# Attention in front of a feed-forward part, moved to the whole tensor array: zero-padded queries, P as the stationary operand, a ones column in V

## The chip, the cores and the metric

The kernel runs on one core of one Trainium2 chip. The metric is device time in microseconds (us), as the median of several executions. PE is the tensor engine (PEld its weight loads), ACT the scalar engine, DVE the vector engine and POOL the engine that issues most loads.

## The reference

There are 8 batches, 8 heads, 576 positions and 64 values a head. Heads 0 to 3 see a local window of 32 positions. Heads 4 to 7 see the earlier positions with the same remainder modulo 32. The attention output, 4608 tokens of 512 values, goes through a bilinear feed-forward part (FFN).

```python
scores = scale * np.matmul(q, k.transpose(0, 1, 3, 2))
mask_local   = (rel >= 0) & (rel < stride)                      # heads 0..3, stride = 32
mask_strided = (rel >= 0) & (pos[None, :] % stride == pos[:, None] % stride)
attn = softmax(where(mask, scores, -1e9));  o = attn @ v        # per batch and head
x = o.transpose(0, 2, 1, 3).reshape(4608, 512)
out = ((x @ w_a) * (x @ w_b)) @ w_out                           # 512 -> 1536 -> 512
```

## The kernel before

The FFN works in 9 tiles of 512 tokens: 12 groups of 8 matmuls (a and b), then 4 groups of 12 (y). pf is the product of a and b. The attention of batch b+1 is cut into steps that are issued between the FFN groups of tile b; the place behind one group is called a slot. A unit is half the positions of one pair of heads, 8 units a batch. Batch 0 has nothing to hide behind and forms the start. The order on PE is fixed by hand.

A head has 64 values, so each attention step used half of the array. Scores contract over 64 rows; transposes and P V write 64 columns. Two heads run beside each other, in the two halves.

```python
def step_S(b, u):                       # scores: two heads in two ROW halves (64*128)
    for i, (k0, q0, g) in enumerate(segs):
        for hh in range(2):
            d0 = 64 * hh
            nc.tensor.matmul(st[:M, hh, i*n:(i+1)*n], lhsT=kT[d0:d0+64, c, k0:k0+M],
                             rhs=qT[d0:d0+64, c, q0:q0+n], start=True, stop=True)
    # ... exp on ACT, mask by a bitwise and on DVE -> p

def step_V(b, u):                       # P V: two heads in two COLUMN halves (128*64)
    for hh in range(2):                 # row sums by a matmul with ones
        nc.tensor.matmul(dn[64*hh:64*hh+64, :W], lhsT=ones[:M], rhs=p[:M, hh], start=True, stop=True)
    # ... o[64*hh:64*hh+64, ...] = matmul(lhsT=vt, rhs=p): x comes out transposed
    nc.scalar.activation(ln, dn[:, :W], ACT.Ln)
    nc.scalar.activation(rc, ln, ACT.Exp, scale=-1.0)      # 1/sum
    nc.vector.tensor_mul(x[:, W*half:W*(half+1)], o[:, :W], rc)
# pools in PSUM: mm 4 banks, st 2, sm 2
```

The softmax here doesn't subtract the row's maximum and nothing guards it: scores larger than these inputs give would overflow.

## Time and profile before

| | before |
|---|---|
| time, median of 4 executions | 375.57 us (375.12 to 375.96) |
| span of the profiled execution | 374.7 us |
| PE busy | 358.7 us, 96% |
| an FFN tile with / without attention beside it | 39.95 / 31.08 us |
| a batch of attention on PE | 8.87 us |
| FFN's first matmul | 25.21 us |

The prediction below shows the lines for most of these rows. A few are from the timeline of PE (start, duration in us, engine, line, operation with its operands, rows*columns of the array in use, number of instructions, in brackets the wait before). The last is from the view of waits (engine, tile and line, what it waited for: us in total, times, longest).

```profile
24.83 0.45 PE L220 MATMUL sm<-p,vs 72*64 72x72 bf16 x8 [0.51 <-ACT ln L224]
...
67.77 0.82 PE L254 MATMUL mm<-xT,wa_sb 128*128 128x512 bf16 x3
69.36 0.38 PE L254 MATMUL mm<-xT,wa_sb 128*128 128x512 bf16 x1 [0.77 <-DVE xT L232]
```

```profile
PE mm L254 <- DVE xT L232: 0.8, 1, 0.8
```

The last P V of batch 0 begins at 24.83 and the FFN follows at 25.21, just 0.38 us later: its first three passes read x of heads 0 to 5, which was multiplied earlier. DVE finishes the last unit's x at 26.03, and the fourth pass, the first that needs it, comes at about 26.5. The wait of 0.8 us is the only long one outside the start. It lies at the boundary of tiles 0 and 1.

### The profile page before, as it was taken

What the parts mean: (1) busy time and instruction counts of PE and PEld (TensorE: products, weight loads), DVE (VectorE), ACT (ScalarE), POOL (GpSimd) and SP (SyncE); (2) the same over time, 40 slices, a digit from 0 to 9 for tenths busy, and PEclk for the clock granted to TensorE, in tenths of its full rate; (3) what the DMA queues carried; (4) which work ended last, traced back from release to release, by engine and by line L of the source; (5) the groups of instructions that cost most, each with busy time, mean ns of one, the idle gap of its engine ahead of it and who ended that gap; (6) DMA issues with size and microseconds to landing.
All of it is one profiled execution on the core that took longest, in us unless ns stands there. A gap on an engine that the chain in (4) does not pass through costs nothing.

```text
span 374.7 us, 7708 instructions
## 1 busy us (share of the span) xinstructions
PE 358.7 (96%) x3217; PEld 173.8 (46%) x3217; DVE 169.7 (45%) x299; ACT 178.6 (48%) x347; POOL 52.3 (14%) x72
## 2 busy tenths in 40 slices
PE   2789999999999999999999999999999999999995
PEld 2544454455444544444444544554445444444442
DVE  2653652465426652556245643655255513312421
ACT  1563764466526652666246643766166623312320
POOL 7833540013001110103000300000000000000000
PEclk9999999999999999999999999999999999999999
DMA  7999999845644194229414843000200020011002
GB/s 114 155 194 197 205 191 191 177 66 37 98 117 65 8 100 117 53 40 103 93 56 66 72 81 99 2 2 19 94 2 3 1 86 28 0 58 56 0 30 84
DMA packets 51730, 29.59 MB, mean 79 GB/s; under 512 B 28400, under 2 KB 47088, under 8 KB 51696
## 3 DMA queue, kind: packets, MB, share of 16 engines
q0 software_dynamic: 46512, 19.67, 43.2%
q1 hardware_dynamic: 5184, 9.44, 6.9%
q8 instruction: 25, 0.41, 0.4%
q14 instruction: 9, 0.07, 0.1%
HBM read 39.31 MB, written 9.44 MB: 130 GB/s over the span
## 4 chain that ended last, share of the span: by engine, by line
PE 93%; DMA 2%; POOL 1%; ACT 1%; DVE 1%; issue 1%; DVEq 0%; POOLq 0%
PE mm L254 52%; PE mm L265 25%; PE sm L166 5%; PE st L194 4%; PE sm L213 4%; PE sm L220 2%; DMA vl<-in_v_dram 2%; POOL k L116 0%; DVE y_sb L271 0%; POOL msl L73 0%; ACT rc L226 0%; DVE xT L232 0%; ACT ln L224 0%; POOL q L116 0%; PE mm L166 0%
## 5 line engine op out<-in xcount | busy, mean ns | idle before, releaser
L259 DVE TENSOR_TENSOR pf<-a_sb,mm 128x512 bf16<-128x512 f32 x108 | 74.3, 688 | 89.9 <-PE mm L254 89.9
L254 PE MATMUL mm<-xT,wa_sb 128*128 128x512 bf16 x432 | 113.6, 386 | 0.8 <-DVE xT L232 0.8
L254 PE MATMUL mm<-xT,wb_sb 128*128 128x512 bf16 x432 | 111.9, 382 | 0.0
L258 ACT COPY a_sb<-mm 128x512 f32<-128x512 f32 x108 | 63.2, 585 | 70.2 <-PE mm L254 70.2
L265 PE MATMUL mm<-wo_sb,pf 128*128 128x512 bf16 x432 | 96.3, 379 | 0.0
L254 PEld LDWEIGHTS <-wb_sb 128*128 128x128 bf16 x432 | 42.6, 99 | 52.9 <-issue 2.9
L265 PEld LDWEIGHTS <-pf 128*128 128x128 bf16 x432 | 40.9, 98 | 47.9
L254 PEld LDWEIGHTS <-wa_sb 128*128 128x128 bf16 x432 | 36.4, 98 | 38.4 <-issue 1.7
L199 ACT ACTIVATE p<-st 128x576 bf16<-128x576 f32 (+1 forms) x64 | 40.7, 635 | 17.5 <-PE st L194 17.4
L224 ACT ACTIVATE ln<-sm 128x288 f32<-128x288 f32 x64 | 26.3, 410 | 29.5 <-PE sm L213 29.5
L269 ACT COPY y_sb<-mm 128x512 f32<-128x512 f32 x18 | 10.5, 585 | 56.3 <-PE mm L265 56.3
L271 DVE COPY y_sb<-mm 128x512 f32<-128x512 f32 x18 | 12.5, 692 | 52.9 <-PE mm L265 52.9
L232 DVE TENSOR_TENSOR xT<-sm,rc 128x288 bf16<-128x288 f32 x32 | 20.4, 639 | 28.4 <-ACT rc L226 27.8
L226 ACT ACTIVATE rc<-ln 128x288 f32<-128x288 f32 x64 | 28.3, 443 | 2.0
L172 ACT COPY qT<-sm 128x576 bf16<-128x576 bf16 x28 | 17.8, 637 | 13.9 <-PE sm L166 13.9
L194 PE MATMUL st<-qT,kT 64*72 64x72 bf16 (+1 forms) x448 | 21.1, 212 | 0.6 <-ACT p L199 0.5
L213 PE MATMUL sm<-p,ones 72*64 72x288 bf16 (+1 forms) x128 | 21.1, 327 | 0.3 <-DVE p L205 0.3
L229 DVE TENSOR_TENSOR xT<-sm,rc 128x288 bf16<-128x288 f32 x32 | 14.6, 458 | 14.2 <-ACT rc L226 12.5
L116 POOL DMA_DIRECT2D q<-in_q_dram x16 | 11.7, 730 | 58.4 <-PE sm L166 53.7
L213 PEld LDWEIGHTS <-ones 72*64 72x64 bf16 (+1 forms) x128 | 7.3, 110 | 24.6 <-issue 21.2
L166 PEld LDWEIGHTS <-q 72*64 72x64 bf16 (+1 forms) x448 | 11.2, 117 | 15.9 <-issue 8.9
L129 POOL DMA_DIRECT2D vl<-in_v_dram x8 | 11.6, 1454 | 45.9 <-PE st L194 45.4
(41 smaller groups left out, 177.8 us busy)
## 6 DMA issues: line engine op xcount, KB each, us to landing
out_dram<-y_sb SPq DMA_DIRECT2D x36, 256.0 KB, 2.0
q<-in_q_dram POOLq DMA_DIRECT2D x16, 288.0 KB, 6.8
k<-in_k_dram POOLq DMA_DIRECT2D x16, 288.0 KB, 7.9
vl<-in_v_dram POOLq DMA_DIRECT2D x7, 384.0 KB, 6.8
vs<-in_v_dram POOLq DMA_DIRECT2D x8, 288.0 KB, 5.8
wa_sb<-in_moe_w_a_dram POOLq DMA_DIRECT2D x4, 384.0 KB, 11.6
wb_sb<-in_moe_w_b_dram POOLq DMA_DIRECT2D x4, 384.0 KB, 11.7
wo_sb<-in_moe_w_out_dram POOLq DMA_DIRECT2D x4, 384.0 KB, 13.5
```

The lines of the kernel that those rows point to most:

```text
L166: nc.tensor.transpose(tp[64 * hh:64 * hh + 64, r, :], src[:, 2 * cc + hh, r, :], ident[:n, :n])
L172: nc.scalar.copy(o, i_)
L194: nc.tensor.matmul(st[:M, hh, i * n:(i + 1) * n], lhsT=kT[d0:d0 + 64, c, k0:k0 + M], rhs=qT[d0:d0 + 64, c, q0:q0 + n], start=True, stop=True)
L199: nc.scalar.activation(p[:M], st[:M, :, :W], ACT.Exp, scale=scale)
L213: nc.tensor.matmul(dn[64 * hh:64 * hh + 64, :W], lhsT=ones[:M], rhs=p[:M, hh], start=True, stop=True)
L224: nc.scalar.activation(ln, dn[:, :W], ACT.Ln)
L226: nc.scalar.activation(rc, ln, ACT.Exp, scale=-1.0)
L232: nc.vector.tensor_mul(dst, o[:, :W].rearrange("d (r p) -> d p r", r=4), rc.rearrange("d (r p) -> d p r", r=4))
L254: nc.tensor.matmul(ps_, lhsT=w[:, f // FC, kk, 128 * (f % FC):128 * (f % FC + 1)], rhs=xT[:, kk, TTOK * t:TTOK * (t + 1)], start=(kk == 0) ...
L258: nc.scalar.copy(a_sb, ab[0])
L259: nc.vector.tensor_mul(pf[:, f, :], a_sb, ab[1])
L265: nc.tensor.matmul(y, lhsT=pf[:, f, 128 * j:128 * (j + 1)], rhs=wo_sb[:, f, :], start=(f == 0), stop=(f == FD - 1))
```

## The change

The intent is that every attention step but the local transposes uses the whole array. Then the array need not change between its modes (whole, row halves, column halves; each change is a gap of 93 to 97 ns in the trace before), and ln and 1/x leave ACT.

- Scores contract over all 128 rows, two heads of k at once, against queries in which the other head's rows are zero (`qz`).
- P becomes the stationary operand and V the moving one, with a 65th column of ones. The output has queries on partitions, and the row sum arrives as column 64.
- Each row is divided by its sum on DVE. The result must then be transposed into x, 28 transposes a batch.
- Strided q and k are transposed 128 values wide. V of the strided heads is loaded in 4 transfers, and buffers are redistributed.

```diff
-    pmm = ... bufs=4     psm = ... bufs=2
+    pmm = ... bufs=3     po = ... bufs=1 (2 banks)     ptp = ... bufs=1
 def step_S
-   matmul(st[:M, hh, ...], lhsT=kT[d0:d0 + 64, c, k0:k0 + M], rhs=qT[d0:d0 + 64, c, q0:q0 + n])
+   matmul(st[:M, j, ...],  lhsT=kT[:, c, k0:k0 + M],          rhs=qz[j][:, c, q0:q0 + n])
 def step_V
-   matmul(dn[...], lhsT=ones[:M], rhs=p[:M, hh])
-   matmul(o[64 * hh:64 * hh + 64, ...], lhsT=vt, rhs=p[:M, hh, i * n:(i + 1) * n])
-   ACT.Ln, ACT.Exp(scale=-1), tensor_mul into xT
+   matmul(ov[:, j, i, :], lhsT=p[:M, j, i * n:(i + 1) * n], rhs=vt)      # vt has D + 1 columns
+   reciprocal(rc, ov[:, :, :, D]);  tensor_mul(xn, ov[:, :, :, 0:D], rc)
+def step_X                                                               # new
+   transpose(tv[:, g, :], xn[:, g], ident)   for 6 or 8 pieces;  scalar.copy into xT
-   pf ... bufs=2;   batch t+1 begins with tile t (batch 1: behind FFN group 3)
+   pf ... bufs=1;   batch b begins two groups before tile b-1 (batch 1: group 2, doubled steps at 3 and 12)
```

More of the change, by code (lines that the diff above doesn't have):

```diff
@@ L20 @@
 PAD = 32
+VW = 80
 FC = 3
@@ L52 @@
     nat = ctx.enter_context(tc.tile_pool(name="nat", bufs=2))
-    kvp = ctx.enter_context(tc.tile_pool(name="kv", bufs=2))
     sb = ctx.enter_context(tc.tile_pool(name="sb", bufs=3))
     fsb = ctx.enter_context(tc.tile_pool(name="ffn", bufs=3))
-    pmm = ctx.enter_context(tc.tile_pool(name="pmm", bufs=4, space=bass.MemoryType.PSUM))
+    pmm = ctx.enter_context(tc.tile_pool(name="pmm", bufs=3, space=bass.MemoryType.PSUM))
     pst = ctx.enter_context(tc.tile_pool(name="pst", bufs=1, space=bass.MemoryType.PSUM))
-    psm = ctx.enter_context(tc.tile_pool(name="psm", bufs=2, space=bass.MemoryType.PSUM))
+    po = ctx.enter_context(tc.tile_pool(name="po", bufs=1, space=bass.MemoryType.PSUM))
+    ptp = ctx.enter_context(tc.tile_pool(name="ptp", bufs=1, space=bass.MemoryType.PSUM))
     nc.scalar.preload_act_table_set("natural_log_exp_and_others")
     ident = const.tile([128, 128], BF16)
-    ones = const.tile([128, 64], BF16)
+    qz_buf = [[const.tile([128, KD, S], BF16, name=f"qz{i}{j}") for j in range(2)] for i in range(2)]
+    vl_buf = [const.tile([128, HL * 6, VW], BF16, name=f"vl{i}") for i in range(2)]
+    vs_buf = [const.tile([NP, HL, RS, VW], BF16, name=f"vs{i}") for i in range(2)]
     mask_l = const.tile([128, 4, LW], I16)
@@ L74, in select, with consts @@
                                 channel_multiplier=cm)
-    def consts():
-        nc.vector.memset(ones, 1.0)
-        nc.vector.memset(msl, -1.0)
-        for kT in kT_buf:
-            nc.vector.memset(kT[:, 0:2, 0:PAD], 0.0)
+    def consts(i):
+        if i == 0:
+            nc.vector.memset(msl, -1.0)
+        nc.vector.memset(kT_buf[i][:, 0:2, 0:PAD], 0.0)
+        for j in range(2):
+            nc.vector.memset(qz_buf[i][j][64 * (1 - j):64 * (2 - j)], 0.0)
+        nc.vector.memset(vl_buf[i][:, :, D:D + 1], 1.0)
+        nc.vector.memset(vs_buf[i][:, :, :, D:D + 1], 1.0)
+        if i == 0:
+            nc.vector.memset(vl_buf[0][:PAD, 0, 0:D], 0.0)
     def mask_local():
@@ L119, in load_vl @@
     def load_vl(b):
-        t = nat.tile([128, HL * 6, D], BF16, tag="vl", name="vl")
+        t = vl_buf[b % 2]
         f = 0
@@ L124, in load_vl @@
             f = 1
-            nc.vector.memset(t[:PAD, 0, :], 0.0)
-            nc.gpsimd.dma_start(out=t[PAD:, 0, :], in_=v[0, 0, 0:LW, :])
+            nc.gpsimd.dma_start(out=t[PAD:, 0, 0:D], in_=v[0, 0, 0:LW, :])
         src = bass.AP(tensor=v.tensor, offset=(b * H * S + LW * f - PAD) * D,
                       ap=[[D, 128], [LW * D, HL * 6 - f], [1, D]])
-        nc.gpsimd.dma_start(out=t[:, f:, :], in_=src)
-        nats[b, "vl"] = t.rearrange("p (h w) d -> p h w d", h=HL)
+        nc.gpsimd.dma_start(out=t[:, f:, 0:D], in_=src)
     def load_vs(b):
-        t = nat.tile([NP, HL, RS, D], BF16, tag="vs", name="vs")
-        nc.gpsimd.dma_start(out=t, in_=v[b, HL:].rearrange("h (p r) d -> p h r d", r=RS))
-        nats[b, "vs"] = t
+        for h in range(HL):
+            nc.gpsimd.dma_start(out=vs_buf[b % 2][:, h, :, 0:D],
+                                in_=v[b, HL + h].rearrange("(p r) d -> p r d", r=RS))
     def load_w(src, dst, c):
@@ L147, in load_wo, with step_T @@
         )
-    qkT = {}
-    def step_T(b, c):
-        if b not in qkT:
-            qkT[b] = (kvp.tile([128, KD, S], BF16, tag="qT", name="qT"), kT_buf[b % 2])
-        R, n = (RS, NP) if c >= 2 else (RL, 96)
-        cc = c % 2
-        for i, nm in enumerate(("q", "k")):
-            src = nats[b, nm, c >= 2]
-            dst = qkT[b][i][:, c, :] if i == 0 else qkT[b][i][:, c, PAD:]
-            if b == 0:
-                tp = pmm.tile([128, R, n], BF16, tag="mm", name="mm")
-            else:
-                tp = psm.tile([128, R, n], BF16, tag="sm", name="sm")
-            for r in range(R):
-                for hh in range(2):
-                    nc.tensor.transpose(tp[64 * hh:64 * hh + 64, r, :], src[:, 2 * cc + hh, r, :], ident[:n, :n])
-            if c < 2:
-                o, i_ = dst.rearrange("d (p r) -> d p r", r=R), tp.rearrange("d r p -> d p r")
-            else:
-                o, i_ = dst, tp.rearrange("d r p -> d (r p)")
-            if i == 0 and b > 0:
-                nc.scalar.copy(o, i_)
-            else:
-                nc.vector.tensor_copy(o, i_)
+    def step_T(b, c, nm):
+        src = nats[b, nm, c >= 2]
+        if b == 0:
+            tp = pmm.tile([128, S], BF16, tag="mm", name="mm")
+        else:
+            tp = ptp.tile([128, S], BF16, tag="tp", name="tp")
+        if c < 2:
+            tv = tp.rearrange("d (r p) -> d r p", r=RL)
+            for r in range(RL):
+                for hh in range(2):
+                    nc.tensor.transpose(tv[64 * hh:64 * hh + 64, r, :], src[:, 2 * c + hh, r, :], ident[:96, :96])
+            perm = lambda t: t.rearrange("d (p r) -> d p r", r=RL)
+            tv = tv.rearrange("d r p -> d p r")
+        else:
+            tv = tp.rearrange("d (g p) -> d g p", p=NP)
+            sv = src.rearrange("p h (q r) d -> p h q (r d)", r=2)
+            for g in range(8):
+                nc.tensor.transpose(tv[:, g, :], sv[:, 2 * (c - 2) + g // 4, g % 4, :], ident[:NP, :NP])
+            perm = lambda t: t
+            tv = tp
+        if nm == "k":
+            nc.vector.tensor_copy(perm(kT_buf[b % 2][:, c, PAD:]), tv)
+        else:
+            for j in range(2):
+                pr = slice(64 * j, 64 * j + 64)
+                nc.scalar.copy(perm(qz_buf[b % 2][j][pr, c, :]), tv[pr])
@@ L176, in unit, with step_Tk, step_Tq @@
+    def step_Tk(b, c):
+        step_T(b, c, "k")
+    def step_Tq(b, c):
+        step_T(b, c, "q")
     def unit(u):
         c, half = u // 2, u % 2
-        if c < 2:
-            ws = range(3 * half, 3 * half + 3)
-            return c, half, 128, LW, [(LW * w, LW * w, w) for w in ws]
-        rs = range(4 * half, 4 * half + 4)
-        return c, half, NP, NP, [(PAD + NP * r, NP * r, r) for r in rs]
+        M, n, G = (128, LW, 3) if c < 2 else (NP, NP, 4)
+        segs = [(G * half + i) * n for i in range(G)]
+        return c, half, M, n, G, segs
@@ L185 @@
     ps = {}
     def step_S(b, u):
-        c, half, M, n, segs = unit(u)
-        qT, kT = qkT[b]
+        c, half, M, n, G, segs = unit(u)
+        kT, qz = kT_buf[b % 2], qz_buf[b % 2]
         st = pst.tile([128, 2, 512], F32, tag="st", name="st")
-        for i, (k0, q0, g) in enumerate(segs):
-            for hh in range(2):
-                d0 = 64 * hh
-                nc.tensor.matmul(st[:M, hh, i * n:(i + 1) * n],
-                                 lhsT=kT[d0:d0 + 64, c, k0:k0 + M],
-                                 rhs=qT[d0:d0 + 64, c, q0:q0 + n],
-                                 start=True, stop=True)
+        for i, q0 in enumerate(segs):
+            k0 = q0 + (0 if c < 2 else PAD)
+            for j in range(2):
+                nc.tensor.matmul(st[:M, j, i * n:(i + 1) * n], lhsT=kT[:, c, k0:k0 + M],
+                                 rhs=qz[j][:, c, q0:q0 + n], start=True, stop=True)
@@ L200, in step_S @@
         if c < 2:
-            mk = mask_l[:, half:half + 3].unsqueeze(1).to_broadcast([128, 2, len(segs), n])
+            mk = mask_l[:, half:half + 3].unsqueeze(1).to_broadcast([128, 2, G, n])
         else:
-            mk = mask_s.unsqueeze(1).unsqueeze(1).to_broadcast([NP, 2, len(segs), n])
+            mk = mask_s.unsqueeze(1).unsqueeze(1).to_broadcast([NP, 2, G, n])
         pi = p[:M].bitcast(I16).rearrange("p t (g n) -> p t g n", n=n)
@@ L206, in step_S @@
         ps[b, u] = p
+    xn = {}
     def step_V(b, u):
-        c, half, M, n, segs = unit(u)
+        c, half, M, n, G, segs = unit(u)
         p = ps.pop((b, u))
-        dn = psm.tile([128, 512], F32, tag="sm", name="sm")
-        for hh in range(2):
-            nc.tensor.matmul(dn[64 * hh:64 * hh + 64, :W], lhsT=ones[:M], rhs=p[:M, hh],
-                             start=True, stop=True)
-        o = psm.tile([128, 512], F32, tag="sm", name="sm")
-        for i, (k0, q0, g) in enumerate(segs):
-            for hh in range(2):
-                h = 2 * (c % 2) + hh
-                vt = nats[b, "vl"][:, h, g, :] if c < 2 else nats[b, "vs"][:, h, g, :]
-                nc.tensor.matmul(o[64 * hh:64 * hh + 64, i * n:(i + 1) * n], lhsT=vt,
-                                 rhs=p[:M, hh, i * n:(i + 1) * n],
-                                 start=True, stop=True)
@@ L223, in step_V @@
-        ln = sb.tile([128, W], F32, tag="ln", name="ln", bufs=2)
-        nc.scalar.activation(ln, dn[:, :W], ACT.Ln)
-        rc = sb.tile([128, W], F32, tag="rc", name="rc", bufs=2)
-        nc.scalar.activation(rc, ln, ACT.Exp, scale=-1.0)
-        x = xT[:, c, S * b:S * (b + 1)]
+        o = po.tile([128, 2, 512], F32, tag="o", name="o")
+        ov = o[:n, :, :G * (D + 1)].rearrange("p j (g e) -> p j g e", e=D + 1)
+        for i in range(G):
+            for j in range(2):
+                if c < 2:
+                    vt = vl_buf[b % 2][:, (2 * c + j) * 6 + 3 * half + i, 0:D + 1]
+                else:
+                    vt = vs_buf[b % 2][:, 2 * (c - 2) + half, 2 * i + j, 0:D + 1]
+                nc.tensor.matmul(ov[:, j, i, :], lhsT=p[:M, j, i * n:(i + 1) * n], rhs=vt,
+                                 start=True, stop=True)
@@ L228, in step_V @@
+        rc = sb.tile([128, 2, 4], F32, tag="rc", name="rc")
+        nc.vector.reciprocal(rc[:n, :, :G], ov[:, :, :, D])
+        if half == 0:
+            xn[b, c] = sb.tile([n, S // n, 2, D], BF16, tag=f"xn{n}", name=f"xn{n}", bufs=2)
+        x = xn[b, c]
         if c < 2:
-            nc.vector.tensor_mul(x[:, W * half:W * (half + 1)], o[:, :W], rc)
+            dst = x[:, 3 * half:3 * half + 3].rearrange("p g j d -> p j g d")
         else:
-            dst = x.rearrange("d (p r) -> d p r", r=RS)[:, :, 4 * half:4 * half + 4]
@@ L232, in step_V @@
-            nc.vector.tensor_mul(dst, o[:, :W].rearrange("d (r p) -> d p r", r=4),
-                                 rc.rearrange("d (r p) -> d p r", r=4))
-    SEQ = (("T0",), ("S0",), ("S1", "T1"), ("V0", "S2"), ("V1", "S3"), ("T2",), ("V2", "S4"),
-           ("V3", "S5"), ("T3",), ("V4", "S6"), ("V5", "S7"), ("V6",), ("V7",))
-    FN = {"T": step_T, "S": step_S, "V": step_V}
+            dst = x[:, :, half, :].rearrange("p (g j) d -> p j g d", j=2)
+        nc.vector.tensor_mul(dst, ov[:, :, :, 0:D], rc[:n, :, :G].unsqueeze(3).to_broadcast([n, 2, G, D]))
@@ new lines, in step_X @@
+    def step_X(b, c):
+        x = xn.pop((b, c))
+        n = LW if c < 2 else NP
+        if b == 0:
+            tp = pmm.tile([128, S], BF16, tag="mm", name="mm")
+        else:
+            tp = ptp.tile([128, S], BF16, tag="tp", name="tp")
+        tv = tp.rearrange("d (g p) -> d g p", p=n)
+        for g in range(S // n):
+            nc.tensor.transpose(tv[:, g, :], x[:, g].rearrange("p j d -> p (j d)"), ident[:n, :n])
+        dst = xT[:, c, S * b:S * (b + 1)]
+        if c >= 2:
+            dst, tv = dst.rearrange("d (p r) -> d p r", r=RS), tv.rearrange("d g p -> d p g")
+        else:
+            tv = tp
+        nc.scalar.copy(dst, tv)
@@ L239, in run @@
+    SEQ = (("Tk0",), ("Tq0",), ("S0", "Tk1"), ("S1", "Tq1"), ("V0", "S2"), ("V1", "S3", "Tk2"), ("V2", "Tq2"),
+           ("V3", "S4", "X0"), ("S5", "Tk3"), ("V4", "X1"), ("V5", "Tq3"), ("S6",), ("S7", "X2"), ("V6",), ("V7",),
+           ("X3",))
+    FN = {"Tk": step_Tk, "Tq": step_Tq, "S": step_S, "V": step_V, "X": step_X}
     def run(b, slot):
         for s in slot:
-            FN[s[0]](b, int(s[1]))
+            FN[s[:-1]](b, int(s[-1]))
     pfs = {}
@@ L247, in ffn_ab @@
         if f == 0:
-            pfs[t] = fsb.tile([128, FD, TTOK], BF16, tag="pf", name="pf", bufs=2)
+            pfs[t] = fsb.tile([128, FD, TTOK], BF16, tag="pf", name="pf", bufs=1)
         pf = pfs[t]
@@ L277 @@
         load_qk(0, False)
-        consts()
+        consts(0)
         make_identity(nc, ident)
@@ L283 @@
         load_vl(0)
-        for slot in (("T0",), ("T1",), ("S0",)):
+        for slot in (("Tk0",), ("Tq0",), ("Tk1",), ("S0",), ("Tq1",), ("S1",)):
             run(0, slot)
@@ L291 @@
         load_qk(1, False)
+        consts(1)
         load_vl(1)
@@ L300 @@
             load_wo(c)
-        for slot in (("S1",), ("T2",), ("V0",), ("S2",), ("V1",), ("S3",), ("T3",), ("V2",),
-                     ("S4",), ("V3",), ("S5",), ("V4",), ("S6",), ("V5",), ("S7",), ("V6",), ("V7",)):
+        for slot in (("Tk2",), ("V0",), ("S2",), ("Tq2",), ("V1",), ("S3",), ("Tk3",), ("V2",), ("X0",), ("S4",),
+                     ("Tq3",), ("V3",), ("S5",), ("V4",), ("X1",), ("S6",), ("V5",), ("S7",), ("V6",), ("X2",),
+                     ("V7",), ("X3",)):
             run(0, slot)
+        slots = []
         for t in range(NT):
-            steps = list(SEQ) if t + 1 < B else []
-            slots = [lambda f=f: ffn_ab(t, f) for f in range(FD)] + [lambda j=j: ffn_y(t, j) for j in range(4)]
-            first = 3 if t == 0 else 0
-            for i, grp in enumerate(slots):
-                grp()
-                if t + 2 < B:
-                    if i == 2:
-                        load_qk(t + 2, False)
-                    elif i == 5:
-                        load_vl(t + 2)
-                    elif i == 8:
-                        load_qk(t + 2, True)
-                    elif i == 11:
-                        load_vs(t + 2)
-                if steps and i >= first:
-                    run(t + 1, steps.pop(0))
+            slots += [(ffn_ab, t, f) for f in range(FD)] + [(ffn_y, t, j) for j in range(4)]
+        todo = []
+        for b in range(1, B):
+            g0 = 2 if b == 1 else 16 * (b - 1) - 2
+            todo.append((b, g0, list(SEQ)))
+        loads = {}
+        for b in range(2, B):
+            g0 = 16 * (b - 2)
+            loads[g0 + 1] = lambda b=b: load_qk(b, False)
+            loads[g0 + 5] = lambda b=b: load_vl(b)
+            loads[g0 + 8] = lambda b=b: load_qk(b, True)
+            loads[g0 + 11] = lambda b=b: load_vs(b)
+        for i, (fn, t, j) in enumerate(slots):
+            fn(t, j)
+            if i in loads:
+                loads[i]()
+            for b, g0, seq in todo:
+                if seq and i >= g0:
+                    run(b, seq.pop(0))
+                    if b == 1 and i in (3, 12):
+                        run(b, seq.pop(0))
 _INS = ['q', 'k', 'v', 'moe_w_a', 'moe_w_b', 'moe_w_out']
```

## The prediction

> **What bounds the kernel now.** I read the page first, then the chain of waits in order of time, then the timeline of PE over one tile of the feed-forward part (FFN), and last the timeline of the first 32 us. From the page:
>
> ```profile
> span 374.7 us, 7708 instructions
> PE 358.7 (96%) x3217; PEld 173.8 (46%) x3217; DVE 169.7 (45%) x299; ACT 178.6 (48%) x347; POOL 52.3 (14%) x72
> ...
> PE 93%; DMA 2%; POOL 1%; ACT 1%; DVE 1%; issue 1%; DVEq 0%; POOLq 0%
> ```
>
> The chain that ends last is 93% PE; DVE and ACT are under half busy. So the time is what PE's stream costs, plus a start and a tail in which PE waits. The chain in order of time splits that stream:
>
> ```profile
> 111.18 1.83 PE mm L254 x8
> ...
> 151.13 1.83 PE mm L254 x8
> ...
> 308.58 20.72 PE mm L254 x96
> 329.30 10.36 PE mm L265 x48
> 339.66 20.72 PE mm L254 x96
> ```
>
> Lines 3 to 5 are a tile with no attention beside it: 339.66 - 308.58 = 31.08 us, 215.8 ns for each of its 144 matmuls. Lines 1 and 2 are the same point of two tiles that do carry a batch: 39.95 us apart. So a batch of attention costs PE 39.95 - 31.08 = 8.87 us, seven times (batches 1 to 7); batch 0 lies in the start. What those 8.87 us consist of is in PE's timeline:
>
> ```profile
> 149.47 1.03 PE L254 MATMUL mm<-xT,wb_sb 128*128 128x512 bf16 x4
> 150.43 0.45 PE L166 MATMUL sm<-ident,q 96*64 96x96 bf16 x12
> 150.71 0.42 PE L166 MATMUL sm<-ident,k 96*64 96x96 bf16 x12
> 151.06 1.04 PE L254 MATMUL mm<-xT,wa_sb 128*128 128x512 bf16 x4
> 151.94 1.03 PE L254 MATMUL mm<-xT,wb_sb 128*128 128x512 bf16 x4
> 152.89 0.30 PE L194 MATMUL st<-qT,kT 64*128 64x96 bf16 x6
> 153.13 1.04 PE L254 MATMUL mm<-xT,wa_sb 128*128 128x512 bf16 x4
> ```
>
> The four matmuls at 149.47 stream until 149.47 + 4 x 0.216 = 150.33; the transposes begin at 150.43. That is some 0.09 us with no stream, and the trace's single records show 93 to 97 ns at every change between full array (128*128), column halves (96*64) and row halves (64*128). With some 20 ns for the first pair's second start, a change costs about 0.11 us. Inside a group two halves run together: pairs start 42 ns apart at 96 columns and 31 to 35 ns at 72. A batch has 33 such changes, about 3.7 us; its streams by pairs make the other 5.1 us. The sum, 8.8, agrees with 8.87.
>
> The start:
>
> ```profile
> 14.00 0.45 PE L220 MATMUL sm<-p,vl 128*64 128x96 bf16 x5 [1.81 <-DMA vl<-in_v_dram]
> ...
> 25.21 1.89 PE L254 MATMUL mm<-xT,wa_sb 128*128 128x512 bf16 x4
> ...
> 26.89 1.91 PE L254 MATMUL mm<-xT,wb_sb 128*128 128x512 bf16 x4
> ```
>
> V of batch 0 lands just before 14.00, and from there to the FFN's first matmul are 11.2 us of a chain PE, ACT, DVE and back for 8 units, 1.4 us a unit. Four FFN matmuls take 1.7 us here against 0.86 later: PE runs at half rate until about 30.7.
>
> [...]
>
> **The change part by part.** I read the order of instructions in the built program, which fixes each engine's queue.
>
> Removed: the 16 matmuls with ones (288 columns) of a batch, ln and 1/x on ACT, most changes of the array's mode. Added: 28 transposes of x a batch, a reciprocal a unit, a second q copy. PE instructions a batch go from 240 to 220.
>
> PE for a batch, warm, all on the full array except the local transposes. [...]score matmuls with 72 weight columns started 35 ns apart with 72 columns to stream, so I estimate 35 for 72 weight columns and 45 for 96.
> - Local transposes, still column halves: 4 groups of 6 pairs at 42.5 plus two changes: 4 x 0.476 = 1.90 us.
> - Strided transposes, now 128 wide: 32 x 32.5 = 1.04.
> - Scores, now one at a time: 24 x 42.5 + 32 x 35 = 2.14.
> - P as weights, V with 65 columns: 24 x 45 + 32 x 35 = 2.20.
> - x transposes: 12 x 42.5 + 16 x 32.5 = 1.03.
> The sum is 8.31 us against 8.87, so 0.56 less, 3.9 us over seven batches. The 25 changes avoided (33 to 8, 2.8 us) are mostly spent again: halves that ran in pairs now run one after the other, and x must be transposed.
>
> ACT loses ln and 1/x (54.6 us), gains q halves and x copies (about 43); DVE gains some 15. Neither becomes the bound in the steady part: the heaviest slots hold about 2.5 us on one engine against about 2.5 of PE.
>
> The start gets longer. The output tile of P V has one buffer (two banks) instead of the two small tiles of before, so unit after unit goes: P V, reciprocal, multiply, next P V. Cold durations: 0.82 us from the first P V matmul to the reciprocal (six loads of 96 columns at 90 ns, plus the 0.37 from a matmul to DVE), 0.2 for the reciprocal (the 72x72 scaling from PSUM took 0.22), 0.06, 0.56 for the multiply ([...]0.69 for the strided units), 0.05. That is 1.7 to 1.9 a unit. Following all four queues in their order from 14.00 (masks of later units and the two q copies sometimes come in front), I get the P V of the 8 units at 14.0, 15.7, 17.4, 19.5, 21.3, 23.2, 25.3 and 27.2, the last x transposes at 29.1, and the FFN at 29.5 against 25.2: plus 4.3 us.
>
> Batch 1 gets waits. Its steps are doubled in slots 3 and 12: scores directly behind the q transposes that they need (two ACT copies, about 1.4 us of PE idle), and two score groups directly behind each other on the one score tile (about 0.8). At the end of tile 0 the next batch's q transposes follow the last x transposes on the one transpose tile (about 0.9). That is 3.1, against 0.9 at the same tile boundary before (the second half of FFN group 0 of tile 1 starts at 69.57 and not 68.63): plus 2.1.
>
> Sum: -3.9 + 4.3 + 2.1 = +2.5 us. From 375.85 that is 378.3. My hand-followed start rests on cold rates for everything and would rather be too long, so I put the middle at 377.5.
>
> **The rivals.** First, the weight loads do not hide behind so short a matmul when both are on the whole array. Then some 170 matmuls a batch cost 20 ns more, 3.5 us a batch, and the time is about 400. Against it: in column halves the loads hide at 72 columns already (next load 1.5 ns after each start, pairs 32.5 apart). Second, the full array is better than I think (P V at 28 ns, columns alone) and the start grows by only 1 or 2 us: then a batch costs 7.7, and with the waits of batch 1 the time is 371. For it: ACT no longer has ln and 1/x between scores in the start. Third, fewer buffers (three banks for FFN instead of four, one for pf, one score, output and transpose tile) stall PE in each tile; 0.1 us a slot would be 1.6 a tile, 11 us in all, 389. Against it: a bank is used again after 2.4 us or more, and its copy takes 0.3 of latency and 0.6. Fourth, V of the strided heads comes in 4 transfers with 128-byte pieces; late weights would stall tile 0. Against it: V of the local heads already has such pieces and lands in 1.97 us (28.48 to 30.45), as fast per byte as the weights, and the last weights land 5 us before their use.
>
> **Range and chances.** The batch term is good to about 0.4 us a batch, 2.8 us; the start to about 2.5; the waits to 1. Together some 4, and the third rival gives the upper side a little more: 372.5 to 382.5. Faster by over 2% (below 368.3) would need the second rival in full and no longer start: 5%. Slower by over 2% (above 383.4) needs one of the stalls: 9%.
>
> **What would show it.** PE's timeline: FFN to scores and P V to scores without the 93 ns; scores 42 and 35 ns apart, one by one; P V 45 and 35. Tile period at the same point: about 39.4 us. The FFN's first matmul at about 29.5. ln and 1/x gone from ACT, no wait for ACT or DVE over 0.2 us on PE from tile 2 on. I am wrong if the period is above 40.5 or below 38.6, if FFN starts before 27, or if PE waits in every tile for copies.

Cut from the recorded text is what no trace or run of this case shows: one paragraph (its measured figures stand elsewhere), the rule for the shortest time of a small matmul, and the formula behind the 0.56 us of a multiply. No term leaves the sum by this. It stands as recorded: -3.9 + 4.3 + 2.1 = +2.5 us, 378.3, with the middle put at 377.5. The 45 ns for 96 weight columns, and with it the 90 at half rate, were the author's estimate; of its kind the trace before has only the 35 ns at 72 weight columns. The 0.56 us can be estimated from that trace: a multiply took 458 ns at 288 columns (L229) and 688 at 512 (L259), which makes 557 at 384. The 20 ns of the first rival are an assumption that no trace shows.

## The result and the profile after

| | before | after |
|---|---|---|
| time, median of 4 | 375.57 us | 377.06 us (376.39 to 377.75) |
| span of the profiled execution | 374.7 | 376.0 |
| PE busy | 358.7 | 353.2 |
| DVE / ACT busy | 169.7 / 178.6 | 182.3 / 174.1 |
| DMA packets | 51730 | 73616 |
| tile with attention | 39.95 | 39.37 |
| FFN's first matmul | 25.21 | 28.05 |

The ratio is 1.004, with a 95% interval of 1.0018 to 1.0063: the change made the kernel 0.4% slower. Ratios are the mean time of one kernel's fast runs over the mean of the other's fast runs of the same rounds, so they are not quite the ratios of the medians. The page of the kernel after (span; busy us and instructions by engine; chain that ended last, by engine):

```profile
span 376.0 us, 7241 instructions
PE 353.2 (94%) x3002; PEld 195.8 (52%) x3057; DVE 182.3 (48%) x366; ACT 174.1 (46%) x287; POOL 72.5 (19%) x96
...
PE 91%; DMA 2%; issue 2%; DVE 2%; POOL 1%; ACT 1%; DVEq 0%; ACTq 0%; POOLq 0%
```

PE is still the bound, but its share of the chain fell from 93% to 91% and DVE's rose from 1% to 2%. So PE got a little work taken off, and a little more waiting. The chain in order of time shows the first part (start, us, engine, tile and line):

```profile
114.46 1.24 PE mm L283 x5
...
153.84 1.24 PE mm L283 x5
```

The same point of two successive tiles lies 39.38 us apart (39.375 to 39.378 by the single records; 39.37 is used below), against 39.95 before. A batch now costs PE 39.37 - 31.08 = 8.29 us. The timeline of PE shows how:

```profile
154.92 0.42 PE L208 MATMUL st<-qz,kT 128*128 128x96 bf16 x6
155.26 0.45 PE L169 MATMUL tp<-ident,k 96*64 96x96 bf16 x12
155.64 1.04 PE L283 MATMUL mm<-xT,wa_sb 128*128 128x512 bf16 x4
...
162.08 0.42 PE L233 MATMUL o<-vl,p 128*96 128x65 bf16 x6
162.34 0.42 PE L208 MATMUL st<-qz,kT 128*128 128x96 bf16 x6
162.59 0.42 PE L176 MATMUL tp<-ident,k 72*128 72x72 bf16 x8
162.85 1.03 PE L283 MATMUL mm<-xT,wa_sb 128*128 128x512 bf16 x3
```

From 162.08 the groups follow each other every 0.26 us with no gap: P V, scores, transposes and FFN share one mode (the last line counts 3 of 4 matmuls; one record is missing). At 154.92 the six scores end after 0.25 us, at 155.17, and the column halves begin only at 155.26. Such gaps are left only around the four local transposes of a batch. The start, from the same view:

```profile
13.82 0.54 PE L233 MATMUL o<-vl,p 128*96 128x65 bf16 x5 [0.64 <-DMA vl<-in_v_dram]
...
25.90 0.69 PE L233 MATMUL o<-vs,p 72*72 72x65 bf16 x8 [0.54 <-DVE xn L244]
27.60 0.66 PE L255 MATMUL mm<-ident,xn 72*128 72x72 bf16 x8 [1.02 <-DVE xn L244]
28.48 1.49 PE L283 MATMUL mm<-xT,wa_sb 128*128 128x512 bf16 x3 [0.22 <-issue]
```

The record of the FFN's first matmul is missing; the group has 4 and the line counts 3. At half rate they are 0.43 us apart (427 ns by the single records here), so the first began at 28.05. Seven units of batch 0 take 25.90 - 13.82 = 12.08 us instead of 24.83 - 14.00 = 10.83. From the last unit to the FFN it is 2.15 us instead of 0.38. The waits of batch 1 beside tile 0:

```profile
39.46 0.20 PE L208 MATMUL st<-qz,kT 128*128 128x96 bf16 x1 [0.72 <-ACT qz L184]
40.12 0.37 PE L208 MATMUL st<-qz,kT 128*128 128x96 bf16 x5 [0.46 <-ACT qz L184]
63.55 0.44 PE L208 MATMUL st<-qz,kT 128*72 128x72 bf16 x8 [0.94 <-ACT p L211]
74.05 0.45 PE L169 MATMUL tp<-ident,q 96*64 96x96 bf16 x12 [0.73 <-ACT xT L261]
```

These are 0.72 + 0.46 + 0.94 + 0.73 = 2.85 us of idle time, against 0.77 before (0.8 in the view of waits). Idle time is counted from the modelled end of the last matmul, which lies later than the point at which the next could have started: the records of 512 columns are 379 ns long in the steady tiles, and their starts 216 apart. From start to start, less the usual spacing, the single records give 0.79 + 0.62 + 1.11 + 0.80 = 3.32 us, against 0.93 before. That is what PE's stream lost, and the prediction measured the wait before in the same way (69.57 - 68.63).

So the sum is -0.58 x 7 = -4.06 for the batches, +2.84 for the start and +2.39 for the waits: +1.17 us. The profiled spans differ by 1.3 and the medians by 1.49. The runs of one kernel scatter by more than what is left.

### The profile page after: what moved, and what is told of

Its sections match the earlier page's. It is cut to its first block, busy times and chain, and to the rows that moved or that the text cites. A ratio compares the mean times of both kernels' runs of the same rounds, so it can differ in the third digit from the quotient of the medians.

```text
span 376.0 us, 7241 instructions
## 1 busy us (share of the span) xinstructions
PE 353.2 (94%) x3002; PEld 195.8 (52%) x3057; DVE 182.3 (48%) x366; ACT 174.1 (46%) x287; POOL 72.5 (19%) x96
## 2 busy tenths in 40 slices
DMA packets 73616, 29.59 MB, mean 79 GB/s; under 512 B 52592, under 2 KB 68976, under 8 KB 73584
## 4 chain that ended last, share of the span: by engine, by line
PE 91%; DMA 2%; issue 2%; DVE 2%; POOL 1%; ACT 1%; DVEq 0%; ACTq 0%; POOLq 0%
PE mm L283 50%; PE mm L294 25%; PE o L233 5%; PE st L208 4%; PE tp L169 3%; PE tp L176 2%; PE tp L255 2%; DMA vl<-in_v_dram 2%; DVE xn L244 1%; ACT p L211 1%; POOL k L125 0%; POOL msl L77 0%; ACT qz L184 0%; DVE p L217 0%; POOL q L125 0%
## 5 line engine op out<-in xcount | busy, mean ns | idle before, releaser
L184 ACT COPY qz<-tp 64x576 bf16<-64x576 bf16 x56 | 35.4, 632 | 27.5 <-PE tp L169 15.5
L244 DVE TENSOR_TENSOR xn<-o,rc 96x384 bf16<-96x384 f32 (+1 forms) x64 | 39.6, 618 | 1.9
L233 PEld LDWEIGHTS <-p 72*72 72x72 bf16 (+1 forms) x448 | 28.8, 127 | 15.8 <-DVE xn L244 2.6
L300 DVE COPY y_sb<-mm 128x512 f32<-128x512 f32 x18 | 12.5, 692 | 45.9 <-PE mm L294 45.9
L208 PE MATMUL st<-qz,kT 128*72 128x72 bf16 (+1 forms) x448 | 29.8, 211 | 2.9 <-ACT qz L184 1.8
L141 POOL DMA_DIRECT2D vs<-in_v_dram x32 | 25.8, 808 | 32.3 <-PE o L233 21.1
L208 PEld LDWEIGHTS <-kT 128*72 128x72 bf16 (+1 forms) x448 | 25.7, 115 | 10.9 <-issue 3.1
L261 ACT COPY xT<-tp 128x576 bf16<-128x576 bf16 x28 | 17.7, 632 | 24.0 <-PE tp L255 24.0
L180 DVE COPY kT<-tp 128x576 bf16<-128x576 bf16 x28 | 16.9, 602 | 14.5 <-PE tp L169 14.5
L236 DVE RECIPROCAL rc<-o 96x6 f32<-96x6 f32 (+1 forms) x64 | 12.2, 191 | 12.6 <-PE o L233 12.5
L217 DVE TENSOR_TENSOR p<-p,mask_s 72x576 int16<-72x576 int16 x32 | 14.4, 450 | 7.0 <-ACT p L211 6.7
## 6 DMA issues: line engine op xcount, KB each, us to landing
wo_sb<-in_moe_w_out_dram POOLq DMA_DIRECT2D x4, 384.0 KB, 10.4
```

Of the source, the lines that this page charges most:

```text
L141: nc.gpsimd.dma_start(out=vs_buf[b % 2][:, h, :, 0:D], in_=v[b, HL + h].rearrange("(p r) d -> p r d", r=RS))
L180: nc.vector.tensor_copy(perm(kT_buf[b % 2][:, c, PAD:]), tv)
L184: nc.scalar.copy(perm(qz_buf[b % 2][j][pr, c, :]), tv[pr])
L208: nc.tensor.matmul(st[:M, j, i * n:(i + 1) * n], lhsT=kT[:, c, k0:k0 + M], rhs=qz[j][:, c, q0:q0 + n], start=True, stop=True)
L233: nc.tensor.matmul(ov[:, j, i, :], lhsT=p[:M, j, i * n:(i + 1) * n], rhs=vt, start=True, stop=True)
L244: nc.vector.tensor_mul(dst, ov[:, :, :, 0:D], rc[:n, :, :G].unsqueeze(3).to_broadcast([n, 2, G, D]))
```

## The experiments

My theory is that the change wins by its fewer mode changes, and loses that again in two places, the start and batch 1. Both lie outside the steady tiles. The rivals are those of the prediction, of which too few buffers is the most serious, and the possibility that what I call a mode change is something else. Twelve kernels ran. All but e_switch were timed against the kernel before in the same rounds, and all gave right results. By the rule of 2% only e_all, e_best and e_warm count as faster, e_best1 is unclear, and the others are the same; smaller differences rest on the intervals and on the traces. "Against after" below means the difference of two ratios times 376 us. The two ratios come from different rounds, so it is good to about 1 us. Differences of medians are named as such.

| run | median us (range) | before, same rounds | ratio, 95% interval |
|---|---|---|---|
| e_halves | 379.63 (379.30–379.90) | 375.64 | 1.0105, 1.0088–1.0122 |
| e_padonly | 379.23 (378.05–379.49) | 375.64 | 1.0089, 1.0070–1.0109 |
| e_switch | 380.45 (one look) | 375.64 | none |
| e_banks | 375.37 (374.91–376.08) | 375.64 | 0.9995, 0.9978–1.0011 |
| e_wide | 372.35 (371.51–372.88) | 376.03 | 0.9897, 0.9874–0.9921 |
| e_sched | 374.19 (373.97–374.58) | 376.03 | 0.9949, 0.9930–0.9969 |
| e_start | 376.14 (375.55–376.49) | 376.03 | 0.9998, 0.9973–1.0023 |
| e_all | 367.45 (367.12–367.59) | 376.03 | 0.9768, 0.9749–0.9787 |
| e_tail | 375.44 (375.37–376.02) | 376.16 | 0.9985, 0.9971–1.0000 |
| e_best | 366.82 (366.27–367.12) | 376.16 | 0.9751, 0.9736–0.9766 |
| e_best1 | 367.83 (366.48–369.44) | 376.16 | 0.9784, 0.9761–0.9806 |
| e_warm | 367.09 (366.15–367.59) | 375.93 | 0.9770, 0.9751–0.9790 |

### e_switch: what a change of mode costs by itself

```diff
# after, behind each FFN group of tiles 7 and 8, which have no attention
+ matmul(d[0:64, 0, 0:32], lhsT=ident[:, 0:64], rhs=ident[:, 0:32])        # column half (t 7, f < 6)
+ matmul(d[:, 0, 0:32], lhsT=ident[0:64, :], rhs=ident[0:64, 0:32])        # row half    (t 7, f >= 6)
+ matmul(d[:, 0, 0:32], lhsT=ident, rhs=ident[:, 0:32])                    # whole array (t 8, f < 6)
```

> The changed kernel with one small extra matmul (32 columns) behind each FFN group of the two last tiles, where no attention runs; its result is not used, the output stays right. Tile 7, groups 0 to 5: into a column half; groups 6 to 11: from a row half; tile 8, groups 0 to 5: whole array; groups 6 to 11: none. My theory: a group takes 1.73 us alone, 1.73 + about 0.03 with a whole-array extra, and 1.73 + 0.2 to 0.25 with a half-array one, column or row alike (two changes and the small matmul). Rival: the idle 0.09 us belongs to small matmuls, or to the weight load behind a long matmul, and not to the mode: then the whole-array extra costs as much as the half-array ones.

From the timeline of PE, in each pair the first matmuls of two successive groups: with a column half between, with a whole-array matmul between, with nothing.

```profile
311.45 1.04 PE L284 MATMUL mm<-xT,wa_sb 128*128 128x512 bf16 x4
313.42 1.04 PE L284 MATMUL mm<-xT,wa_sb 128*128 128x512 bf16 x4
...
345.12 1.02 PE L284 MATMUL mm<-xT,wa_sb 128*128 128x512 bf16 x4
346.87 1.02 PE L284 MATMUL mm<-xT,wa_sb 128*128 128x512 bf16 x4
...
355.61 1.03 PE L284 MATMUL mm<-xT,wa_sb 128*128 128x512 bf16 x4
357.33 1.03 PE L284 MATMUL mm<-xT,wa_sb 128*128 128x512 bf16 x4
```

By the single records, all of five or six repeats within 0.004, a group takes 1.727 us plain, 1.753 with a small whole-array matmul, 1.967 with a column half and 1.95 with a row half. The small matmul itself costs 0.025 us. The same matmul in another mode costs 0.225 to 0.24, so the two changes cost 0.1 us each. That is what the prediction took from the profile.

### e_halves: scores back on row halves, all else as after

```diff
- lhsT=kT[:, c, k0:k0 + M],  rhs=qz[j][:, c, q0:q0 + n]
+ lhsT=kT[pr, c, k0:k0 + M], rhs=qz[j][pr, c, q0:q0 + n]      # pr: the 64 rows of head j
```

> The changed kernel, with its score matmuls put back on row halves (64 rows of kT and of the padded query tile; copies, zeroing and everything else as it is). My theory (a change of the array's mode costs 0.11 us, two halves run at the price of one): the score streams of a batch fall from 24 x 42 + 32 x 35 ns = 2.13 us to half, minus 1.06; 14 changes of mode come back (one in each of the 2 slots that also hold local transposes, two in each of the other 6), plus 1.58. Net plus 0.52 us a batch: the tile period goes from 39.37 to 39.9 us, and the time to 380.7 us (plus 3.6, the start within 1 us of as it is). Rival: changes of mode cost little and the lost pairing is what made the change fail; then the period falls to 38.3 and the time to some 370 us.

```profile
159.94 0.42 PE L234 MATMUL o<-vl,p 128*96 128x65 bf16 x6
160.29 0.30 PE L209 MATMUL st<-qz,kT 64*128 64x96 bf16 x6
160.53 1.04 PE L284 MATMUL mm<-xT,wa_sb 128*128 128x512 bf16 x4
```

The six scores take 0.24 us up to the FFN, change included: two heads run beside each other again. But P V to scores is now 0.35 us and not 0.26. The tile period is 39.84 us, 0.47 more than after (0.52 expected). Padding the queries therefore pays 0.47 us a batch in the changed kernel. The time rose by 2.6 us (medians) rather than by the 7 x 0.47 = 3.3 that the batches alone make. In its profiled run the FFN also began 0.2 us earlier, and the half-rate stretch behind that was 4.1 us against 5.5, which gives back some 0.7.

### e_padonly: zero-padded queries alone, in the kernel before

```diff
- matmul(st[...], lhsT=kT[d0:d0 + 64, c, k0:k0 + M], rhs=qT[d0:d0 + 64, c, q0:q0 + n])
+ matmul(st[...], lhsT=kT[:, c, k0:k0 + M],          rhs=qT[hh][:, c, q0:q0 + n])
+ # q copied into two zero-padded tiles, memsets of these ahead of all else on DVE
```

> The kernel before, with the zero-padded queries alone: scores on the whole array, q copied in two halves into zeroed tiles, all else as before. My theory: streams plus 1.06 us a batch, changes of mode from 33 to 24 (minus 1.02): the tile period stays at 39.95 to 40.0, time 375.6 to 377 us (the start may grow by up to 1 us through four more copies on DVE). Rival one: padding pays by itself, because it removes a change at each score group; then minus 2 us or more. Rival two: padding only costs, 7 us.

The tile period was 40.06 us, 0.11 more than before, so padding alone gains nothing there. The working gives about the same. By the order of the steps it saves only 9 changes a batch (0.9 us), because P V and the transposes beside the scores stay on column halves. Running the heads one after the other costs about 0.13 to 0.14 us in each of 8 score groups (3 more starts at 42.5 ns, or 4 at 35), 1.1 us. Together with e_halves this shows that the parts of the change depend on each other: padded scores paid where their neighbours use the whole array too, and not beside column halves.

The time missed my expectation: 379.23 us. That is in part my edit's own fault. Four memsets of 1.02 us each stood ahead of the mask's memset on DVE. POOL waited for that before it issued the load of V, P V went on at 14.84 instead of 14.00, and the FFN began at 27.40, 2.2 us late. So V explains 0.84 of it; the rest was not traced, and the added q copies stand on DVE in that stretch. Its period may be read, its time not.

### e_banks: the kernel before with as few buffers as after

```diff
- pmm bufs=4, pf bufs=2
+ pmm bufs=3, pf bufs=1
```

> The kernel before with the changed kernel's FFN buffers: three PSUM banks for FFN instead of four and one pf tile instead of two, all else as before. My theory: nothing in the tiles, period 39.95, time within 0.7 us of before; the start, whose first transposes share these banks, may move by some tenths. Rival: fewer banks make PE wait 0.1 us a slot, 1.6 us a tile, 11 us in all.

The ratio is 0.9995 and the period 39.95 us as before. Three banks for the FFN and one pf tile cost nothing, so this part of the third rival falls. The single score, output and transpose tiles were not in this run: from tile 2 on PE waits for no copy in the kernel after, but the pace of the start comes from the output tile (see e_start), and the 0.73 us at the end of tile 0 from the transpose tile. The score tile was single before, too.

### e_wide: the last mode changes removed

Local q and k of batches 2 to 7 are loaded head by head, so that two heads lie side by side. Then 6 whole-array transposes replace 12 on column halves.

```diff
+ for h in range(HL): dma_start(out=tw[:, h // 2, :, h % 2, :], in_=src[b, h].rearrange("(p r) d -> p r d", r=R))
- for hh in range(2): transpose(tv[64 * hh:64 * hh + 64, r, :], src[:, 2 * c + hh, r, :], ident[:96, :96])
+ transpose(tv[:, r, :], src[:, c, r].rearrange("p j d -> p (j d)"), ident[:96, :96])
```

> The changed kernel, with its local transposes on the whole array too from batch 2 on: q and k of the local heads are loaded head by head (8 transfers instead of 2) so that the two heads of a pair lie side by side, and 6 transposes of 128 weight columns take the place of 12 of 64. My theory: each of the 4 groups of a batch falls from 0.476 us (6 pairs at 42 ns, two changes of mode) to 6 x 42.5 = 0.255; minus 0.88 us a batch, tile period from 39.37 to 38.5, minus 5.3 us over six batches: about 371.8 us, below the kernel before. Rival: the time of these groups is not the change of mode, or the smaller pieces and the added transfers come too late and PE waits for them; then no gain, or a loss.

```profile
151.19 0.42 PE L176 MATMUL tp<-ident,q 96*128 96x96 bf16 x6
151.45 1.03 PE L293 MATMUL mm<-xT,wa_sb 128*128 128x512 bf16 x4
```

A transpose group costs 0.26 us in place of 0.48. The period is 38.48 us (38.5 expected), 0.89 less a batch. The time fell to 372.35 us; against after that is 5.4 us, where 6 x 0.89 = 5.3. Here the model of modes predicted a time, and the time came.

### e_sched: the waits of batch 1

```diff
- g0 = 2 if b == 1 ...;  a second step at groups 3 and 12
+ g0 = 1 if b == 1 ...;  a second step at group 13; last x transposes of batch 1 into an FFN bank
```

> The changed kernel, with batch 1 begun one FFN group earlier and only one slot doubled (group 13: second half of the scores of the last head pair with the x transposes, then P V of the unit before), so that no step directly follows what it needs; the last x transposes of batch 1 go into an FFN bank. My theory: the 0.72 + 0.46, 0.94 and 0.73 us that PE waits in tile 0 of the changed kernel fall away: minus 2.8 us, about 374.2. Rival: they come back as waits for the loads of batch 1, which now is wanted earlier, or for DVE: less than 1 us gained.

The four waits shown above are gone from tile 0, the FFN starts at 28.16, and the time is 374.19 us where 374.2 was expected. By medians this is 2.9 us less than after, by the ratios 3.4. What the waits had cost PE's stream is 3.3 us.

### e_start: a second place for the output of P V in batch 0

```diff
- o = po.tile([128, 2, 512], F32, ...)
+ o = pmm.tile(...) if b == 0 and half == 1 else po.tile(...)
```

> The changed kernel, with a second output place for P V in batch 0 alone: the second unit of each pair writes to FFN banks that stand idle then (local units one bank, strided units two, with reciprocal and multiply split in two); the later q and k transposes of batch 0 use the transpose tile. My theory: the one output tile sets the pace of the start (P V, reciprocal, multiply, next P V); with two, FFN begins at 26 to 26.5 instead of 28.05: minus 1.5 to 2 us. Rival: ACT (exp, two q copies, x copy: 1.6 us a unit) or DVE sets that pace anyway: less than 0.5 us, or even later through the split multiplies.

```profile
14.15 0.53 PE L244 MATMUL o<-vl,p 128*96 128x65 bf16 x5 [0.95 <-DMA vl<-in_v_dram]
...
25.19 0.69 PE L244 MATMUL mm<-vs,p 72*72 72x65 bf16 x8
26.57 0.93 PE L269 MATMUL mm<-ident,xn 72*128 72x72 bf16 x8 [0.69 <-DVE xn L258]
27.31 0.62 PE L297 MATMUL mm<-xT,wa_sb 128*128 128x512 bf16 x1
```

The units of batch 0 now run from 14.15 to 25.19 us, 11.04 for seven against 12.08 after and 10.83 before. The single output place was what slowed the pace. But the FFN began at 27.31, and not at 26 to 26.5: V landed 0.3 us later in this run, and from the last unit to the FFN it was still 2.12 us. I had counted that tail as part of the pace. The time was 1.6 us less than after, within what was expected, but in part by luck: the repair took 1.1 us off the way from the first unit to the FFN (14.23 - 13.16), V's late landing gave back 0.3, and in the profiled run the half-rate stretch was 3.8 us instead of 5.5, worth another 0.9, which the edit did not aim at.

### e_tail: FFN work ahead of the last transposes

```diff
# after, group 0 of tile 0
+ a: passes kk 0..2;  X3 of batch 0;  b: passes kk 0..2;  a: kk 3;  b: kk 3
```

> The changed kernel with the first three passes of the first FFN group issued before the transposes of x of batch 0, which close the start, and the rest of that group interleaved with the second group of its tile. Theory (the tail is part of what the change costs: between the last P times V and the first FFN matmul lie 2.15 us, against 0.38 us before): three cold FFN passes of some 0.43 us fill 1.1 to 1.3 us of the stretch in which the PE waits for the last normalized rows; the time falls by about 1.1 us, to about 376.0. Rival (the tail hides the clock's warm-up, which merely moves): less than 0.3 us.

```profile
26.81 1.06 PE L286 MATMUL mm<-xT,wa_sb 128*128 128x512 bf16 x2 [0.22 <-issue]
27.66 0.68 PE L255 MATMUL mm<-ident,xn 72*128 72x72 bf16 x8
```

Three FFN passes (the first one's record is missing) fill the stretch from 26.38 to 27.66, while the last rows are normalized. The last transposes begin no later than before (27.66 against 27.60). The time is 2.1 us less than after, where 1.1 was expected. In its profiled run full rate came at 30.17, that is 3.8 us after the first FFN pass; after it was 33.6, 5.5 us. Half of the difference, 0.9 us, would explain the rest, but the two were not separated.

### e_all, e_best, e_best1: the repairs together

e_all is e_wide, e_sched and e_start in one kernel; e_best adds e_tail.

> All three together. If they add up as my theory says, minus 5.3, minus 2.8 and minus 1.5: about 367.5 us, 2.1% faster than the kernel before. If the start does not move: about 369.

The three differences against after add up to -0.0143 - 0.0091 - 0.0042 = -0.0276, which makes a ratio of 0.9764. Measured were 0.9768 and 367.45 us.

> The kernel with the wide local transposes from batch 2 on, batch 1 begun earlier and the second output place in batch 0 (367.45 us), with the split first FFN group added. If the gain of the split adds to the others: about 366.4; if the stretch is already filled by the earlier start: 367.2 to 367.5.

The split gained 0.0017, or 0.6 us, between the two expectations. In the profiled run the FFN began at 25.7 instead of 27.2, but full rate came at 31.6 instead of 30.5. At 366.82 us and a ratio of 0.9751 this is the fastest of all kernels run. It beats the kernel before by 2.5% and the kernel after by 2.9% (0.9751 / 1.004).

```diff
- if b >= 2 and not strided:      # e_best1: the wide loads from batch 1 on
+ if b >= 1 and not strided:
```

> The same, with wide local transposes from batch 1 on. Theory (each batch is worth 0.88 us on the PE): about 0.9 us less than the kernel with them from batch 2 on. Rival (batch 1's loads, now more and smaller pieces in the start, come late or push the weights back, whose slack is 3 to 4 us): no gain, or a loss, and the waits of the PE for DMA in tile 0 show it.

The view of waits of e_best1:

```profile
PE mm L317 <- DMA wb_sb<-in_moe_w_b_dram: 0.8, 1, 0.8
```

The rival was right. With batch 1's smaller pieces the FFN waits 0.8 us for the weights, a wait that e_best does not have, and the 0.88 us are gone. The median is even 1 us higher, the runs scatter over 3 us, and the verdict is unclear; no gain is what it shows.

### e_warm: full rate before the start

```diff
# e_best, ahead of everything on PE
+ for _ in range(14): matmul(wm, lhsT=wz[:, 0:128], rhs=wz)      # 512 columns each
```

> The kernel with all four repairs (366.82 us) and, ahead of everything on the PE, 14 matmuls of 512 columns on a constant tile, about 6 us of work at half rate in a stretch in which the PE waits for the first queries and keys (7.58 us). Theory (the stretch of half rate that follows the FFN's start, 3 to 7 us long in the runs so far, depends on what the PE did before it, and the small matmuls of the start don't end it): the FFN's first matmuls come out 216 ns apart instead of 427, which saves half of the stretch, 1.7 to 3.5 us, and the start's own PE work, about 9 us at half rate, gets shorter where the PE is what it waits for, up to 1 us more: 362.5 to 365.0. Rival (full rate is lost again in the pauses between 8 and 14 us): no change, 366.3 to 367.3, or a little more if the 14 matmuls hold up the first transposes.

```profile
12.05 0.23 PE L254 MATMUL o<-vl,p 128*96 128x65 bf16 x1 [0.19 <-DVE p L227]
13.91 0.53 PE L254 MATMUL o<-vl,p 128*96 128x65 bf16 x5 [1.63 <-DMA vl<-in_v_dram]
14.26 0.67 PE L218 MATMUL st<-qz,kT 128*128 128x96 bf16 x6
```

Full rate comes while these matmuls run. By single records they are 427 ns apart up to 5.34 us and 216 from 5.76. The small groups that follow run at full rate until 12 us (0.42 us for 12 transposes at 8.14, against 0.68 in e_best). Then PE waits 1.63 us for V, and from 13.91 on everything is at half rate again, up to 29.8. The early gain is spent at that wait: P V goes on at 13.91, in e_best at 14.02. The wait isn't shown to be what ended full rate: the granted clock is 1.00 from 12.3 to 12.5 us and 0.50 from 12.7 on, so it fell some 0.3 us into the wait. In e_best PE is busy for 10.4 of the 11.5 us from 14 to 25.5, and its small matmuls stay at half rate too (0.67 us for six scores); what would have raised the rate there is not shown. The time is that of e_best within the scatter (0.9770 against 0.9751), so the rival was right in the outcome. The stretches of half rate behind the FFN's start are 2.5 (e_padonly) to 5.9 us (e_best) by the records, and not 3 to 7 as I had written. The page lists this execution with a granted clock of 0.976, because here the record marks the half-rate stretch as 0.5 (14 to 25.5 us reads 0.50; in e_best the same stretch reads 1.00, though its matmuls come at the same pace). Its time, 366.15, is in line with the others.

## Why the prediction was right or wrong

**Right: the direction and the range; the middle in part by luck.** 377.5 us were predicted and 377.06 measured, inside the range and within 2% either way. That the middle lies only 0.44 off is partly luck. The start was written 1.46 too long and the waits 0.3 too short, the sum began from the one profiled time (375.85) where the median was 375.57, and 0.8 was taken off by judgement.

**Right: the batch.** The step said 8.31 us instead of 8.87, and 8.29 was measured. Scores came 42.5 and 35 ns apart, local P V 45 once it ran, and strided P V 35, as estimated. The claim that the mode changes avoided are mostly spent again on heads run one after the other is shown by e_padonly (all spent) and e_halves (padding worth only 0.47 us a batch). e_wide shows that 0.89 us a batch was left to gain.

**Right in mechanism, off in size: the start.** The step was "plus 4.3 us", and 2.84 was measured. Its terms can be compared. A unit was taken as 1.7 to 1.9 us, in the list of starts 13.2 / 7 = 1.89, and it took 12.08 / 7 = 1.73. That is the mis-sized term: 1.1 us of the 1.46 by which the step was off. Part of it lies between a unit's first P V matmul and its reciprocal, written as 0.82 us with loads 90 ns apart; it took 0.72 to 0.73 in four of the units, and local P V came 80 ns apart. The multiply was right (551 and 686 ns on average, 0.56 and 0.69 written). The first P V was 0.18 us earlier than assumed, and the tail took 2.15 us where 2.3 was written. The doubt stated in the text, that cold rates for everything make the start too long, was right, and the middle was moved by less than it deserved. e_start shows that the single output tile sets most of the pace. e_tail shows that the tail was exposed.

**Right: the waits.** 3.1 us were predicted, as 1.4, 0.8 and 0.9, and PE's stream lost 1.41, 1.11 and 0.80, together 3.3. So the net is +2.39 against +2.1 (3.1 less 0.9 would be 2.2; the text rounded down). e_sched removed them, and the time fell by 2.9 to 3.4.

**The rivals.** The 20 ns more a matmul for weight loads on the whole array did not come: score matmuls are 42.5 ns apart with 128 weight columns to load for each, and P V 45 ns with 96, as the main estimate had it. The records of these loads are 103 and 132 ns long on average, so they overlap the matmuls. Matmuls with 128 weight columns and 72 moving came 32 ns apart; those with 96 and 65 came 45, and those with 72 and 65 came 35, both slower with fewer columns of either kind. Whether padding P to 128 columns would pay was not tried. The shorter start fell too; it grew by 2.84. Too few buffers fell as a stall in every tile: e_banks shows it for the FFN's, and no wait over 0.2 us for a copy appears on PE from tile 2 on. The single output tile in the start and the single transpose tile at the end of tile 0 did cost, as the main estimate had it. The late weights fell for the kernel after, whose first FFN weights land at 22.1 us (before 18.3) and the last at 56.5, used at 59.6. With e_best1's additional pieces that rival comes true.

**What stays open.** Of the 1.3 us between the profiled spans 0.1 is not assigned, of the 1.49 between the medians 0.3, less than the scatter. The length of the half-rate stretch behind the FFN's start, 2.5 to 5.9 us in the profiled runs, differs from kernel to kernel in a way that I could not steer, and it moves a time by up to half of that difference. Between before and after it is the same within 0.2 us (5.4 and 5.5). The clock records grant full rate from 30.53 us on before and from 33.60 on after. What sets that moment was not shown.

## What to carry to other kernels

Here packing two half-size matmuls into one array was worth the streaming time that it saved minus the changes of mode around it. A change beside whole-array work cost 0.1 us, as much as two of the small matmuls (42.5 ns), so count changes, and convert neighbours together or not at all. The latency of an extra stage (here normalize, then transpose) cost nothing beside the FFN tiles, where from tile 2 on no wait over 0.2 us for a copy appears on PE, though its transposes still took PE's time, about 1 us a batch (12 at 42.5 ns, 16 at 32). At the start, where nothing hid it, it counted: 2.15 us from the last unit to the FFN instead of 0.38. So look there for the gain that a steady-state count promises and the total doesn't show. Once the sum has named the losses, each can be mended by itself, and here the mended gains added up to within 0.0004 of the ratio.
